# Operand sums of a Strassen product moved from GpSimd to VectorE, a third tile pair for high and low words, and a new order for the attention stage

## The chip, the cores and the metric

The kernel runs on one core of a Trainium2 chip. The metric is the time of one execution on the device, in microseconds (us). Five engines work side by side, each through its own list of instructions in a fixed order: TensorE (PE, with its weight loads shown as PEld), VectorE (DVE), ScalarE (ACT), GpSimd (POOL) and SyncE (SP), which here only starts transfers (DMA). An instruction waits at the head of its list until what it needs is there, and everything behind it on that engine waits with it.

## The reference

Three parts, one behind the other. In NumPy, cut to what matters:

```python
# 1. attention with hashed buckets: q, k, v are 2 x 8 x 768 x 64, proj is 64 x 6
q_bits, k_bits = (q @ proj > 0), (k @ proj > 0)              # 6 bits each -> a bucket number
mask   = q_bucket[:, :, :, None] == k_bucket[:, :, None, :]
scores = where(mask, q @ k.T / 8, -1e9)
attn   = exp(scores - rowmax);  attn /= attn.sum(-1) + 1e-9
x = (attn @ v)  -> 1536 tokens x 512
# 2. gated layer: w1, w2 512 x 1024, w3 1024 x 1024, w_out 1024 x 512
x = ((x @ w1) * (x @ w2)) @ w3 @ w_out
# 3. four experts, mixed by p = domain_probs / sum: e1 4 x 512 x 1024, e2 4 x 1024 x 512
out = sum_e p[:, e] * (relu(x @ e1[e]) @ e2[e])
```

## The kernel before

Every float32 operand of a matmul is cut into a high word (a copy rounded to the type that TensorE reads fast) and a low word (the rest), and a product is three matmuls: high by high, high by low, low by high. The high word is an ACT copy (`hi_of`, line 155), the low word a DVE subtraction (`lo_of`, line 158), or either on POOL (`pool_hi`, 161; `pool_lo`, 164).

No engine order is written out by hand. Each step is an `op(key, engine, duration, function, dependencies, priority)`, and `emit_all` walks all steps with a list planner: each engine takes, of what is ready by the planned durations, the step with the lowest priority number. `RANK`, a table with a number for each kind of step of the attention stage, is added to the priorities; `LAT` holds the planned delays from engine to engine. What comes out is each engine's fixed list. So a changed number in `RANK`, in `LAT` or in a planned duration moves instructions but adds none.

**Attention** (about the first 272 us). 16 heads, each of three units of 256 queries. A unit is: two score matmul groups into one of two PSUM tiles `s_ps`; the row minimum of the negated scores on DVE, which also copies them to SBUF (`e`, line 426); the exponential on ACT (429); a small sum on POOL and a reciprocal on DVE (442, 444); the scaling on POOL or ACT (438, 439); three rounds of transposes on PE into `t_ps` (460), high words on ACT (466) and low words on DVE (468); the product with v into `pv_ps`; an ACT copy (485) and a DVE sum (487) into the token tile `xa`. Each head is prepared ahead (`head`, 324 to 362): q and k rows are loaded into `r`, scaled and cut on POOL (`hh`, `ll`), and copied by DMAs into `ka`, `kb` and `hh`; v is loaded into `rv`, in rows of 64 numbers, and cut on POOL. The hash bits come from a matmul (`bits_of`), a comparison on DVE (`is_pos`, 377) and, for all heads but the first, DMAs (400, 402) that put them under the scores' operands, where they act as the mask. For head 0 the comparisons write straight to the operands (`first_head`: keys `mk` and `mq`).

Beside the attention the weights of part 2 are prepared (`conv64`, 181 to 216): they come as 64-bit numbers, a raw tile `wraw` of 512 KB each (196), and an ACT instruction (198) and five DVE instructions make one float32 half tile of them in `cbuf`; the first eight halves are then cut on ACT and POOL, the later ones on ACT and DVE. ACT's instruction of line 198 waits for the landing of its raw tile. When enough of the first 512 tokens is done, 96 matmuls of part 2 fill gaps of TensorE at the end of the stage.

**Parts 2 and 3** (from 274 us). TensorE runs twelve matmuls a group: gate products, then `w3` by `w_out`, then the layer H in three blocks of 512 tokens. Each of a block's eight groups of H needs one pair of high and low words in a ring of two tiles (`hl`). Block 0 lands in the PSUM tiles `o_ps`, block 1 in `u_ps`, block 2 in `o_ps`. Part 3 multiplies the first two blocks by a Strassen scheme of seven products (`mul`, products m = 1 to 7); five of these need sums or differences of quarters of H's output. In the kernel before, ACT copies all of blocks 0 and 1 from PSUM to the SBUF tiles `G` (eight copies), and POOL makes ten sums of 128 x 512 from them (line 859: two for each of the products 4, 3, 1, 7, 6) into `cbuf`; ACT and DVE then cut each sum into high and low words (`split`). This happens while TensorE runs block 2 (470 to 500 us). In the same stretch POOL also cuts expert weights (161, 164, tiles of 128 x 1024). The four experts follow.

## Time and profile before

| | us |
|---|---|
| runs (median of 3; 1002.5 to 1004.2) | 1002.8 |
| the profiled execution | 1005.64 |
| its span in the trace | 1003.9 |
| PE busy | 977.6 (97%) |
| DVE busy | 662.0 (66%) |
| ACT busy | 432.4 (43%) |
| POOL busy | 313.4 (31%) |

PE is idle for 26.3 us of the span. The page's slices show which engines are full where: in the first quarter (attention) DVE and ACT are nearly as full as PE, and the transfers are dense in the first 50 us; from there on PE alone is full, but for the slice from 477 to 502 us. The granted clock of TensorE is at its full level, 2.4 GHz, in all slices. Times of rows count from the start of the span; `[0.71 <-PE s_ps L149]` at a row's end says that the engine stood idle for 0.71 us ahead of it and what ended that.

### The profile page before, as it was taken

What the parts mean: (1) busy time and instruction counts of PE and PEld (TensorE: products, weight loads), DVE (VectorE), ACT (ScalarE), POOL (GpSimd) and SP (SyncE); (2) the same over time, 40 slices, a digit from 0 to 9 for tenths busy, and PEclk for the clock granted to TensorE, in tenths of its full rate; (3) what the DMA queues carried; (4) which work ended last, traced back from release to release, by engine and by line L of the source; (5) the groups of instructions that cost most, each with busy time, mean ns of one, the idle gap of its engine ahead of it and who ended that gap; (6) DMA issues with size and microseconds to landing.
All of it is one profiled execution on the core that took longest, in us unless ns stands there. A gap on an engine that the chain in (4) does not pass through costs nothing.

```text
span 1003.9 us, 13346 instructions
## 1 busy us (share of the span) xinstructions
PE 977.6 (97%) x4939; PEld 822.7 (82%) x4939; DVE 662.0 (66%) x1194; ACT 432.4 (43%) x779; POOL 313.4 (31%) x297
## 2 busy tenths in 40 slices
PE   7899999999999999999799999999999999999998
PEld 6788888988788888888588888888888888888886
DVE  6799999998499984954965444554445544455343
ACT  5789999988533332434422221222212222122121
POOL 6777788764000000041641204212042120421000
PEclk9999999999999999999999999999999999999999
DMA  5853554321033331320210101101011010100012
GB/s 159 192 130 79 130 122 107 93 61 42 1 105 121 124 113 39 109 84 1 63 43 26 38 1 57 49 26 39 0 59 48 27 37 1 57 28 21 1 50 77
DMA packets 51137, 64.13 MB, mean 64 GB/s; under 512 B 17688, under 2 KB 34072, under 8 KB 51072
## 3 DMA queue, kind: packets, MB, share of 16 engines
q1 hardware_dynamic: 50928, 63.27, 22.1%
q8 instruction: 39, 0.64, 0.3%
q14 instruction: 26, 0.21, 0.1%
q10 hardware_dynamic: 144, 0.01, 0.0%
...
## 4 chain that ended last, share of the span: by engine, by line
PE 73%; DVE 18%; ACT 3%; issue 2%; DMA 2%; POOL 1%; SPq 0%; DVEq 0%; ACTq 0%
PE u_ps L149 50%; PE o_ps L149 19%; DVE et L468 5%; DVE e L426 5%; PE t_ps L149 2%; DMA r<-in_qk 1%; ACT e L429 1%; DVE xa L487 1%; PE pv_ps L149 1%; PE t_ps L460 1%; PE s_ps L149 1%; ACT et L466 1%; DVE hl L158 1%; DVE xh L158 1%; DVE hl L876 1%
## 5 line engine op out<-in xcount | busy, mean ns | idle before, releaser
L149 PE MATMUL u_ps<-xh,slot 128*128 128x512 f32 x768 | 179.9, 389 | 1.2 <-DVE xh L158 1.2
L149 PE MATMUL o_ps<-slotl,hl 128*128 128x512 f32 x768 | 178.2, 390 | 0.4 <-DVE hl L876 0.2
L149 PEld LDWEIGHTS u_ps<-xh,slot 128*128 128x128 f32 x768 | 144.1, 188 | 31.5 <-DVE xh L158 1.6
L149 PEld LDWEIGHTS o_ps<-slotl,hl 128*128 128x128 f32 x768 | 143.9, 188 | 31.5 <-DVE hl L876 1.7
L881 DVE TENSOR_TENSOR m<-m,u_ps 128x512 f32<-128x512 f32 x96 | 62.9, 683 | 138.4 <-ACT m L155 114.7
L161 POOL TENSOR_SCALAR slot<-wraw 128x1024 fp32r<-128x1024 f32 x16 | 17.3, 1080 | 384.6 <-DVE slotl L158 184.1
L149 PE MATMUL u_ps<-xh,slotl 128*128 128x512 f32 x480 | 111.6, 389 | 0.0
L149 PEld LDWEIGHTS u_ps<-xh,slotl 128*128 128x128 f32 x480 | 90.1, 188 | 18.7
L468 DVE TENSOR_TENSOR et<-t_ps,et 128x512 fp32r<-128x512 f32 x144 | 96.5, 680 | 5.3 <-ACT et L466 4.7
L429 ACT ACTIVATE e<-e,sm 128x768 f32<-128x768 f32 x96 | 89.6, 934 | 12.3 <-DVE e L426 10.8
L426 DVE TENSOR_SCALAR_CACHE_REDUCE e<-s_ps 128x768 f32<-128x768 f32 x96 | 90.3, 945 | 4.3 <-PE t_ps L460 3.1
L149 PE MATMUL pv_ps<-et,vv 128*128 128x256 f32 x576 | 91.8, 295 | 0.9 <-DVE xa L487 0.7
L460 PE MATMUL t_ps<-ident,e 128*128 128x128 f32 x576 | 85.6, 276 | 6.7 <-DVE et L468 4.8
L466 ACT ACTIVATE et<-t_ps 128x512 fp32r<-128x512 f32 x144 | 83.0, 593 | 12.5 <-PE t_ps L460 5.8
L149 PE MATMUL u_ps<-slotl,hl 128*128 128x512 f32 x384 | 87.7, 389 | 0.0
L149 PEld LDWEIGHTS u_ps<-slotl,hl 128*128 128x128 f32 x384 | 72.1, 188 | 15.0
L460 PEld LDWEIGHTS t_ps<-ident,e 128*128 128x128 f32 x576 | 65.2, 140 | 16.9 <-DVE et L468 7.9
L149 PEld LDWEIGHTS pv_ps<-et,vv 128*128 128x128 f32 x576 | 75.0, 190 | 3.4 <-DVE xa L487 2.8
L439 POOL TENSOR_SCALAR e<-e,sm 128x768 f32<-128x768 f32 x72 | 65.7, 921 | 18.4 <-DVE sm L444 15.0
L155 ACT ACTIVATE m<-u_ps 128x512 f32<-128x512 f32 x32 | 19.1, 598 | 107.0 <-PE u_ps L149 107.0
L873 ACT ACTIVATE hl<-m 128x512 fp32r<-128x512 f32 x32 | 20.3, 633 | 92.3 <-DVE m L881 92.3
L876 DVE SCALAR_TENSOR_TENSOR hl<-gl,hl 128x512 fp32r<-128x512 f32 x32 | 23.8, 742 | 54.3 <-ACT hl L995 46.2
...
## 6 DMA issues: line engine op xcount, KB each, us to landing
...
```

Of the source, the lines that this page charges most:

```text
L149: nc.tensor.matmul(out=o, lhsT=l, rhs=r, start=start, stop=stop)
L155: nc.scalar.activation(out=dst, in_=ps, func=AF.Copy)
L158: nc.vector.tensor_tensor(out=dst, in0=ps, in1=f(hi), op=ALU.subtract)
L426: op(("mx", u, t), "DVE", 873, lambda ps=ps, m=m, e=e: nc.vector.tensor_scalar(out=e, in0=ps[:, 0:S], scalar1=THR, scalar2=None, op0=ALU.m ...
L429: op(("ex", u, t), "ACT", 921, lambda e=e, m=m, rs=rs: nc.scalar.activation(out=e, in_=e, func=AF.Exp, scale=-1.0, bias=m, accum_out=rs), ...
L439: return "POOL", 872, lambda: nc.gpsimd.tensor_scalar(out=e, in0=e, scalar1=r[:, t:t + 1], scalar2=1.0, op0=ALU.mult, op1=ALU.mult)
L460: nc.tensor.transpose(out=ps[:, k, t * 128:(t + 1) * 128], in_=e_t[2 * (u % ER) + t][:, kt * 128:(kt + 1) * 128], identity=ident)
L466: op(("hi", n), "ACT", 480, lambda ps=ps, et=et: nc.scalar.activation(out=et[:, 0], in_=ps, func=AF.Copy), [("T", u, j), ("pv", n - NET)], Tj)
L468: op(("lo", n), "DVE", 602, lambda ps=ps, et=et: nc.vector.tensor_tensor(out=et[:, 1], in0=ps, in1=f(et[:, 0]), op=ALU.subtract), [("hi", ...
L873: op(key, "ACT", 480, lambda: nc.scalar.activation(out=hl_t[n % 2][:, 0], in_=m_t[m], func=AF.Relu), after, clock[0])
L876: op(key, "DVE", 602, lambda: nc.vector.scalar_tensor_tensor(out=hl_t[n % 2][:, 1], in0=src(), scalar=0.0, in1=f(hl_t[n % 2][:, 0]), op0=A ...
L881: nc.vector.tensor_tensor(out=out, in0=a, in1=b, op=o)
```

## The change

- **Sums.** The operand sums of products 4, 3, 1, 7 and 6 are made by DVE. One operand is read straight from the PSUM tile in which H's block lies (`hb`), the other from `G`. Product 4's two sums read block 0's PSUM tile and come during block 1, the other eight read block 1's and come during block 2. ACT copies six quarters to `G` instead of eight. The sums' tiles are `m_t` and `cbuf`, and part 3's products wait for all reads of `u_ps` (`u_in`).
- **Third tile.** The ring `hl` of high and low words has three tiles in part 3; parts before it still use two.
- **v.** The input array v is laid out ahead of the launch so that each partition's row is one piece of 384 numbers (1.5 KB), not six of 64.
- **First mask bits.** For head 0 the second comparison is cut in two, 256 and 512 columns, and the first score group waits for the first piece alone; head 1's low words (key `l`) come behind it.
- **Order.** 32 of the 34 numbers of `RANK` are new, planned durations of transfers are longer (raw tiles 2700 for 1460, heads 2000 for 1130, copies 1000 for 700) with a planned delay of 1900 for 2300, and some planned DVE and ACT durations are longer. The third head's load also waits for more of head 0's steps.

```diff
-    "S0": -59.56,
+    "S0": -145.18,
...
-            ("SP", 1460, [("cd", n - NRAW), ("c2", n - NRAW)], "cl",
+            ("SP", 2700, [("cd", n - NRAW), ("c2", n - NRAW)], "cl",
...
-        "SP": {"PE": 2300, "ACT": 2300, "DVE": 2300, "POOL": 2300, "SP": 2300, "NONE": 0},
+        "SP": {"PE": 1900, "ACT": 1900, "DVE": 1900, "POOL": 1900, "SP": 1900, "NONE": 0},
...
-                op(("l", hh), "DVE", 870, lambda: scaled_lo(nc.vector), [("h", hh)], T, g)
+                op(("l", hh), "DVE", 1000, lambda: scaled_lo(nc.vector), [("h", hh), ("mq", 0)], T, g)
...
-        op(("lv", hh), "SP", 600, lambda: nc.sync.dma_start(out=rv, in_=v[b, h].rearrange("(k p) d -> p k d", p=128)),
+        op(("lv", hh), "SP", 1000, lambda: nc.sync.dma_start(out=rv, in_=v[b, h].rearrange("p (k d) -> p k d", k=NK)),
...
-        op(("mq", 0), "DVE", 865, lambda: is_pos(lo[64:64 + PC], ps, q), [("mk", 0)], T, "b0")
-        keys[("sf", n)] = keys[("mq", 0)]
+        for i, (key, c) in enumerate(((("mq", 0), slice(0, 256)), (("sf", n), slice(256, S)))):
+            op(key, "DVE", (330, 600)[i], lambda c=c: is_pos(lo[64:64 + PC, c], ps, q, c), [("mk", 0)], T + i, "b0")
...
-        hl_t.extend(tiles(2, [128, 2, 512], "hl", F32R, lp))
+        hl_t.extend(tiles(3, [128, 2, 512], "hl", F32R, lp))
...
+    def hl(n):
+        return hl_t[n % (2 if n < KF * NB else 3)]
...
-    def xs(m):
-        return f(cbuf[:, (4, 3, 1, 7, 6).index(m) % 2])
+    def xs(m, k):
+        return m_t[k + (0 if m == 3 else 2)] if m in (1, 3) else f(cbuf[:, m == 6, k])
...
-        for d in range(KM):
-            op(("hl", blk, d), "ACT", 480, lambda blk=blk, d=d, hb=hb: hi_of(G[blk][:, d], hb[d]),
-               [("H", blk, KF - 1)] + [("gdone", 0, ff) for ff in range(KF)], T)
...
+        kept_d, first_d, m0 = ((0, 1, 2, 3), 0, 2) if blk == 0 else ((2, 3), 2, 5)
+        for d in kept_d:
+            op(("hc", blk, d), "ACT", 480, lambda blk=blk, d=d, hb=hb: hi_of(G[blk][:, d], hb[d]), done, T)
...
-        for m, a, b, o in ((4, x21, x11, ALU.subtract), (3, x12, x22, ALU.subtract), (1, x11, x22, ALU.add),
-                           (7, x21, x22, ALU.add), (6, x11, x12, ALU.add)):
+        sums = ((4, 2, (0, 0), ALU.subtract),) if blk == 0 else (
+            (3, 0, (1, 2), ALU.subtract), (1, 2, (0, 0), ALU.add), (7, 2, (0, 2), ALU.add), (6, 0, (0, 0), ALU.add))
...
-                op(("xs", m, k), "POOL", 1225, lambda m=m, a=a, b=b, o=o, k=k: nc.gpsimd.tensor_tensor(
-                    out=xs(m)[:, k], in0=G[a[0]][:, a[1] + k], in1=G[b[0]][:, b[1] + k], op=o),
+                op(("xs", m, k), "DVE", 602, lambda m=m, a=a, b=b, c=c, o=o, k=k, hb=hb: nc.vector.tensor_tensor(
+                    out=xs(m, k), in0=hb[a + k], in1=G[b][:, c + k], op=o),
```

**What stands in the engines' lists.** Three places follow, before and then after. Number suffixes are buffers.

VectorE, the start of the program: `ll_82` and `ll_83` are the low words of heads 0 and 1, `kb_90` and the 12-row `ll_82` the two comparisons of head 0, `e_96` the first row minimum. Before:

```order
L330 SCALAR_TENSOR_TENSOR ll_82<-r_111,svec,hh_78 128x768
L330 SCALAR_TENSOR_TENSOR ll_83<-r_112,svec,hh_79 128x768
L377 TENSOR_SCALAR kb_90<-s_ps_126,thr,amp 12x768
L377 TENSOR_SCALAR ll_82<-s_ps_126,thr,amp 12x768
L426 TENSOR_SCALAR e_96,sm_119<-s_ps_127 128x768
```

After:

```order
L331 SCALAR_TENSOR_TENSOR ll_82<-r_111,svec,hh_78 128x768
L378 TENSOR_SCALAR kb_90<-s_ps_126,thr,amp 12x768
L378 TENSOR_SCALAR ll_82<-s_ps_126,thr,amp 12x256
L378 TENSOR_SCALAR ll_82<-s_ps_126,thr,amp 12x512
L331 SCALAR_TENSOR_TENSOR ll_83<-r_112,svec,hh_79 128x768
L428 TENSOR_SCALAR e_96,sm_119<-s_ps_127 128x768
```

Head 1's low words moved from ahead of both comparisons to behind them, and the second comparison is two instructions.

ScalarE, around the first instruction that reads a raw weight tile (`cbuf<-wraw_68`). Before it is row 26 of ACT's list, its load row 20 of SP's:

```order
L429 ACTIVATE e_98,sm_123<-e_98,sm_123 128x768
L466 ACTIVATE et_105<-t_ps_129 128x512
L429 ACTIVATE e_99,sm_123<-e_99,sm_123 128x768
L198 ACTIVATE cbuf<-wraw_68 128x512
L466 ACTIVATE et_104<-t_ps_129 128x512
```

After it is row 57, its load row 37:

```order
L468 ACTIVATE et_102<-t_ps_131 128x512
L487 ACTIVATE pvs_107<-pv_ps 64x256
L468 ACTIVATE et_103<-t_ps_129 128x512
L199 ACTIVATE cbuf<-wraw_68 128x512
L431 ACTIVATE e_96,sm_122<-e_96,sm_122 128x768
```

The instruction moved back by 31 rows and its load by 17.

VectorE in the last block of H: `hl` are low words for H's groups, `xh`, `slot` and `slotl` the low words of Strassen operands, `cbuf`, `m` the sums. Before:

```order
L158 TENSOR_TENSOR hl_3029<-xa,hl_3029 128x512
L158 TENSOR_TENSOR xh_3019<-gl_3027,xh_3019 128x512
L158 TENSOR_TENSOR xh_66<-cbuf,xh_66 128x512 x2
L158 TENSOR_TENSOR xh_3019<-cbuf,xh_3019 128x512
L158 TENSOR_TENSOR hl_3030<-xa,hl_3030 128x512
L158 TENSOR_TENSOR xh_3019<-cbuf,xh_3019 128x512
L158 TENSOR_TENSOR hl_3029<-gl_3028,hl_3029 128x512
L158 TENSOR_TENSOR slot_62<-cbuf,slot_62 128x512
L158 TENSOR_TENSOR hl_3030<-gl_3028,hl_3030 128x512
```

After:

```order
L158 TENSOR_TENSOR hl_3031<-xa,hl_3031 128x512
L158 TENSOR_TENSOR xh_3020<-gl_3028,xh_3020 128x512 x2
L158 TENSOR_TENSOR xh_3020<-m_3034,xh_3020 128x512
L158 TENSOR_TENSOR hl_3030<-xa,hl_3030 128x512
L864 TENSOR_TENSOR m_3035<-u_ps_3041,gl_3028 128x512
L158 TENSOR_TENSOR slot_62<-m_3036,slot_62 128x512
L158 TENSOR_TENSOR slot_62<-m_3037,slot_62 128x512
L158 TENSOR_TENSOR xh_3020<-m_3035,xh_3020 128x512
L158 TENSOR_TENSOR hl_3031<-xa,hl_3031 128x512
L864 TENSOR_TENSOR cbuf<-u_ps_3042,g_67 128x512
L864 TENSOR_TENSOR cbuf<-u_ps_3043,g_67 128x512
L158 TENSOR_TENSOR hl_3030<-gl_3029,hl_3030 128x512
```

Eight sums (line 864) now stand in this list between H's low words; two subtractions, those of product 4, left it for block 1.

## Rows read from the trace of the kernel before

**Rows 1.** Waits of PE: engine, line, releaser: us in total, times, longest us.

```profile
PE o_ps L149 <- DVE hl L158: 5.2, 5, 1.5
PE o_ps L149 <- DVE hl L876: 0.2, 1, 0.2
```

**Rows 2.** Busy us by stretch: us, PE, PEld, DVE, ACT, POOL, PEclk, DMA share, GB/s.

```profile
25.00:50.00 25.00, 20.58 (x148) 18.54 (x147) 19.84 (x43) 19.25 (x39) 19.86 (x23) 1.00 0.85 194
100.00:150.00 50.00, 48.66 (x355) 44.31 (x354) 49.52 (x107) 46.73 (x93) 40.16 (x48) 1.00 0.52 125
350.00:400.00 50.00, 50.00 (x222) 41.40 (x222) 31.09 (x58) 13.28 (x23) 0.00 (x0) 1.00 0.23 74
450.00:500.00 50.00, 44.85 (x193) 35.48 (x192) 36.00 (x37) 22.14 (x38) 22.85 (x13) 1.00 0.09 25
260.00:265.00 5.00, 5.00 (x29) 4.38 (x28) 1.79 (x4) 0.58 (x2) 0.00 (x0) 1.00 0.00 0
```

**Rows 3.** Timeline of the start: start us, us, engine, line, operation [idle before]; then one tile's group.

```profile
8.02 0.28 PE L149 MATMUL s_ps<-ll,pbh 128*128 128x256 f32 x1
9.92 1.08 DVE L377 TENSOR_SCALAR kb<-s_ps,thr,amp 12x768 fp32r<-12x768 f32 x1
11.03 1.07 DVE L377 TENSOR_SCALAR ll<-s_ps,thr,amp 12x768 fp32r<-12x768 f32 x1
12.81 0.96 DVE L426 TENSOR_SCALAR_CACHE_REDUCE e<-s_ps 128x768 f32<-128x768 f32 x1 [0.71 <-PE s_ps L149]
...
L330 DVE SCALAR_TENSOR_TENSOR ll<-r,svec,hh x2: 1019/1699/2379, 6.4 to 7.5; 128x768 fp32r<-128x768 f32 x2
```

**Rows 4.** Timeline, 15 to 42 us: POOL, then DVE after its long gaps.

```profile
15.83 0.90 POOL L351 TENSOR_SCALAR r<-r,svec 128x768 f32<-128x768 f32 x1
17.11 1.84 POOL L164 TENSOR_TENSOR ll<-r,hh 128x768 fp32r<-128x768 f32 x1
19.34 2.68 POOL L439 TENSOR_SCALAR e<-e,sm 128x768 f32<-128x768 f32 x3
22.35 0.17 DVE L444 RECIPROCAL sm<-sm 128x2 f32<-128x2 f32 x1 [2.04 <-POOL sm L442]
33.51 0.43 DVE L200 TENSOR_SCALAR cbuf<-cbuf 128x512 f32<-128x512 f32 x1 [1.67 <-ACT cbuf L198]
41.84 0.96 DVE L426 TENSOR_SCALAR_CACHE_REDUCE e<-s_ps 128x768 f32<-128x768 f32 x1 [2.78 <-PE t_ps L460]
```

**Rows 5.** Timeline: raw tile loads on SP, ACT's first reads of them, DVE behind.

```profile
26.34 0.43 SPq L196 DMA_DIRECT2D wraw<-in_w  x1
32.79 0.68 ACT L198 ACTIVATE cbuf<-wraw 128x512 f32<-128x512 f32 x1 [1.47 <-DMA wraw<-in_w]
62.50 0.37 SPq L196 DMA_DIRECT2D wraw<-in_w  x1
68.24 0.67 ACT L198 ACTIVATE cbuf<-wraw 128x512 f32<-128x512 f32 x1 [2.12 <-DMA wraw<-in_w]
69.43 0.69 DVE L468 TENSOR_TENSOR et<-t_ps,et 128x512 fp32r<-128x512 f32 x1 [1.73 <-ACT et L466]
```

**Rows 6.** Timeline in and behind the last block of H: POOL and DVE.

```profile
478.44 2.85 POOL L164 TENSOR_TENSOR slotl<-wraw,slotl 128x1024 fp32r<-128x1024 f32 x1
478.96 2.88 DVE L158 TENSOR_TENSOR xh<-cbuf,xh 128x512 fp32r<-128x512 f32 x1
481.25 6.82 POOL L859 TENSOR_TENSOR cbuf<-g,gl 128x512 f32<-128x512 f32 x4
502.44 2.64 DVE L881 TENSOR_TENSOR m<-m,u_ps 128x512 f32<-128x512 f32 x4 [0.54 <-PE u_ps L149]
503.25 2.41 POOL L164 TENSOR_TENSOR slot<-wraw,slot 128x1024 fp32r<-128x1024 f32 x1
```

**Rows 7.** Stretches of half a microsecond, columns as in the second group.

```profile
165.00:165.50 0.50, 0.50 (x5) 0.50 (x5) 0.50 (x1) 0.48 (x3) 0.50 (x1) 1.00 0.99 395
205.00:205.50 0.50, 0.50 (x7) 0.50 (x6) 0.50 (x3) 0.50 (x2) 0.00 (x0) 1.00 0.96 219
```

More of the change, by code (lines that the diff above doesn't have):

```diff
@@ L27 @@
     "CP": 16.1,
[L28 to L59 removed]
+    "S0": -145.18,
+    "S1": -25.65,
+    "T0": -239.96,
+    "T1": -102.2,
+    "T2": -154.22,
+    "b0": 25.44,
+    "b1": -195.19,
+    "bits": -112.79,
+    "en": -239.65,
+    "ex0": 16.57,
+    "ex1": -26.35,
+    "fd": -190.81,
+    "fx": 57.64,
+    "hi0": 26.3,
+    "hi1": -174.65,
+    "hi2": -42.43,
+    "ld": -147.73,
+    "lo0": 1.38,
+    "lo1": -154.39,
+    "lo2": -137.92,
+    "lv": -113.67,
+    "mx0": -252.86,
+    "mx1": -28.91,
+    "p0": -23.78,
+    "p1": -102.39,
+    "po": -95.03,
+    "prep": -35.61,
+    "pv": -23.28,
+    "r1": -46.45,
+    "r2": -72.09,
+    "v": 25.95,
+    "xa": -161.97,
 }
@@ L675, in take_hl @@
         nh[0] += 1
[L676 removed]
+        return n, ([("hf", n - (2 if n < KF * NB + 2 else 3))] if n > 1 else sw)
     def down(key, n, lhs, rhs, first, last, after, ps=None):
@@ L849, in split @@
             op(("xd", m, k), "DVE", 602, lambda: lo_of(bx(m)[:, 1, k], src(), bx(m)[:, 0, k]), [("yh", m, k)], TX)
+        done = [("H", blk, KF - 1)] + [("gdone", 0, ff) for ff in range(KF)]
+        kept_d, first_d, m0 = ((0, 1, 2, 3), 0, 2) if blk == 0 else ((2, 3), 2, 5)
+        for d in kept_d:
+            op(("hc", blk, d), "ACT", 480, lambda blk=blk, d=d, hb=hb: hi_of(G[blk][:, d], hb[d]), done, T)
         for k in range(2):
-            split(m, k, lambda blk=blk, d=d + k: G[blk][:, d], [("hl", blk, d + k)] + after)
@@ L927, in go @@
                         mm(u_ps[n % 4], lhs()[:, a, k], bx(m)[:, b, k], i == 0, i == 5)
-                op(("M", e, fp, m), "PE", 6 * 227, go, free_ + after + [("xd", m, k) for k in range(2)], clock[0])
+                op(("M", e, fp, m), "PE", 6 * 227, go, free_ + u_in + after + [("xd", m, k) for k in range(2)], clock[0])
                 clock[0] += Q / 2
@@ L944, in tile_lsh_attention_moe @@
                 n, got = mul(m, lhs, have_u)
-                op(("uf", n), "ACT", 480, lambda n=n, x=x: hi_of(m_t[x], u_ps[n % 4]), got + prev, clock[0])
+                op(("uf", n), "ACT", 480, lambda n=n, x=x: hi_of(m_t[x], u_ps[n % 4]), got + prev + [("xd", 3, k) for k in range(2)], clock[0])
                 keys[key(f"t{m}")] = keys[("uf", n)]
```

111 lines of the change are left out of this document (41 added, 70 removed).

## The prediction

> **What bounds the kernel now.** I read the waits of PE first, since PE is the fullest engine, then the busy times by stretch, then the timeline wherever a stretch showed gaps. Two stretches lose time.
>
> From 274 us on PE is the bound and full: 350 to 400 us shows 50.00 busy of 50, 222 matmuls, so one is 50 / 222 = 0.225 us and a group of twelve 2.70 us [rows 2]. The one hole is 450 to 500 us, with 44.85 busy [rows 2]: PE waits there five times, 5.2 us in sum, for DVE's line 158, H's low words [rows 1]. DVE is late because it advances in step with POOL: a DVE subtraction of 128 x 512 started at 478.96 and took 2.88 us, ending 0.55 us behind a POOL instruction that ran from 478.44 for 2.85 us; POOL's sums follow each other at 6.82 / 4 = 1.70 us [rows 6].
>
> In the attention stage PE shows busy, but DVE sets the pace: from 100 to 150 us DVE is busy 49.52 of 50 and PE 48.66 [rows 2]. Before 72 us DVE has holes. Four are long: 2.04, 1.67 and 2.78 us [rows 4] and 1.73 us [rows 5]; with the slow start, they are what can be gained there, because behind 72 us DVE has hardly any. At the end PE takes over: 260 to 265 us shows PE 5.00 of 5 and DVE 1.79 [rows 2].
>
> **The change part by part.** The profiled execution took 1005.6 us, its span 1003.9 and 1.7 around it; the median of the runs is 1002.8, so I carry a difference over to that, 2.8 us lower. The granted clock is at full in every stretch [rows 2] and gets no term.
>
> *First mask bits.* Bits of head 0 leave PE at 8.02 + 0.28 = 8.30. In the kernel before DVE first makes head 1's low words, 2.38 us against 1.02 for head 0's, and starts the comparisons at 9.92 and 11.03; the first row minimum comes at 12.81 [rows 3]. After, the comparisons can start at 8.35: 1.11 us for the first (the step from 9.92 to 11.03), some 0.40 and 0.75 for the two pieces of the second (a third and two thirds of 1.07, and an instruction's fixed part). Scores run on PE from 9.9 on, beside the rest. Then come head 1's low words, 1.02 to 2.38 us by the two rows, and the first minimum, at 11.6 to 13.0. POOL is at work there too, so I take 1.3 us: 11.9, a gain of 0.9 (bounds -0.2 and 1.2). Their copy to `ka` on SP comes later, behind two loads of q, k and one of v; nobody needs it before head 1's scores.
>
> *POOL at the first units.* DVE's reciprocal at 22.35 waited 2.04 us for a POOL addition, which stood behind three scalings from 19.34 on, and these behind head 2's subtraction (17.11, 1.84 us) and head 3's first scaling (15.83, 0.90 us) [rows 4]. In POOL's new list head 3's scaling stands behind the first of the three, so this one starts at least 0.9 us earlier; it can't return more than the 2.04. I take 1.3 (0.9 to 2.0).
>
> *Raw weight tiles.* ACT waited 1.47 us for the first tile, loaded at 26.34 and read at 32.79, and 2.12 us for the third, loaded at 62.50 and read at 68.24; DVE behind it 1.67 [rows 4] and 1.73 us [rows 5]. A load so takes up to 6.4 us in this stretch. The order after has the first load 17 places later on SP and its reader 31 places later on ACT, the second load three rows behind it and its reader at ACT's row 65. The load's predecessor on SP copies head 5's low words; when these were done in the trace, ACT stood near row 35, 22 rows ahead of the new reader, and a row of ACT is 46.73 / 93 = 0.50 us [rows 2]: some 11 us, enough. I book 1.5 of the 1.67 (1.2 to 1.7) and 1.5 of the 1.73 (0.5 to 1.7; I compared the rows of the first two tiles alone). What was hidden by these holes comes due later: DVE has the same 40 instructions of conversion in its list before the last sum of attention in both orders, so nothing is added.
>
> *Copies of head 3.* The 2.78 us at 41.84 [rows 4] end when the first score of head 3 is there, whose bits and copies waited in transfers: DMA is 0.85 busy from 25 to 50 us [rows 2]. What leaves this queue is one 512 KB tile, and v costs less: 196.6 KB of v in 256-byte rows move at 219 / 0.96 = 228 GB/s, 0.86 us, loads with 2 and 3 KB rows at 395 / 0.99 = 399 GB/s, 0.49 us for v and 1.3 us for the tile [rows 7]. So about 1.7 us of traffic go from ahead of the copies, against six small transfers on SP that stay as they were. I take 1.3 (0 to 2.5).
>
> Sum of attention: 0.9 + 1.3 + 1.5 + 1.5 + 1.3 = 6.5 us (2.4 to 9.1). Does it reach the end? Behind 72 us DVE works without holes through the same instructions, plus one, so its stream keeps the lead; at 230 us PE takes over with as many matmuls as before, of which 38 instead of 51 are left behind the last product with v. Seven of DVE's conversion instructions stand behind the 82nd of 96 row minima instead of ahead of it, where DVE has gaps: up to 7 x 0.65 = 4.5 us more, not booked, since PE is at 48.66 of 50 and can hardly go faster.
>
> *Sums on DVE.* POOL loses ten instructions of 1.70 us, ACT two copies. DVE gets ten of 0.66 us, if a sum with an operand in PSUM costs what line 881's do: four of them took 2.64 us while POOL subtracted beside them [rows 6]. In block 2 (eight groups, 8 x 2.70 = 21.6 us) DVE then has 8 low words, 10 subtractions, 8 sums and five small ones, 26 x 0.66 + some 2 = 19 us: it fits. The low words for the group after next have 2.70 us less an ACT copy and a subtraction (0.68 + 0.69 [rows 5]) and the handovers between the engines, some 0.4: 0.9 us of slack. Two expert weight tiles are still cut on POOL in this block. If a 2.85 us subtraction of them holds up H's low words, it costs PE 2.85 - 0.9 = 1.95 us each time, if not, nothing: 0 to 3.9 us remain, I take 2.3. The stage gains 5.2 - 2.3 = 2.9 us (1.3 to 5.2). Part 3's products wait for all reads of `u_ps`; the last sum stands two low words ahead of the group before which the first product runs, so this wait is covered; uncovered it would cost one sum, 0.7 us.
>
> *Third tile.* PE's wait for part 3's low words is 0.2 us [rows 1]; I book 0.2 (0 to 0.4).
>
> Total 6.5 + 2.9 + 0.2 = 9.6 us: 1005.6 - 9.6 = 996.0 for a profiled execution, **993.2** for the median.
>
> **The rivals.**
> 1. *POOL's weight cuts take the place of its sums.* The rows show one DVE subtraction held for the whole of a POOL instruction [rows 6]. If both remaining tiles meet H's low words, the stage keeps 3.9 us: 993.2 + 1.6 = 994.8. For it: the tiles become due by H's groups, in the middle of the block. Against: in the rows the DVE instruction started 0.52 us behind POOL's; started ahead it would have run. On this the Trainium skill, "SBUF — State Buffer", section "SBUF: two separate sides", says that VectorE with two SBUF inputs and GpSimd hold a port pair in turn, for a whole instruction, whoever starts first. By that rule the 3.9 us come about only if POOL starts first both times, and the trace agrees for the one case (2.88 us, where a subtraction of this size takes 0.69).
> 2. *The early holes come back elsewhere.* Transfers stay dense, the first minimum gets its 13.0, the copies of head 3 still arrive late, and the new lists put small waits in. Attention gains 1 us instead of 6.5: 993.2 + 5.5 = 998.7. For it: DMA at 0.85 [rows 2]. Against: two of the four holes are ACT waiting for a raw tile, and these the order plainly removes.
> 3. *Slower: the reciprocal waits for POOL in every head.* In the new lists DVE's reciprocal must find POOL's addition done; POOL makes a head's low words in 1.84 us at one piece, and where the addition is queued behind it DVE stands, as at 22.35, where it cost 2.04 us [rows 4]. 13 heads follow. At 0.9 us a head (11.7 us) the gain of 9.6 is gone by more than 2; at 1.1 us a head it is 993.2 + 14.3 = 1007.5. For it: nearly all priorities are new and DVE has no slack. Against: POOL's new list keeps the addition's place around the low words (subtraction, addition, scaling) as in the old one, and such a wait came only three times before.
> 4. *No change*: attention loses about 2 us in new waits instead of gaining 6.5 and the H stage gains what it should: 1002.8 + 2 - 3.1 = 1001.7.
>
> **How the numbers follow.** Two runs of this kernel differ by about 0.2%, 2.0 us, so faster means below 1000.8 and slower above 1004.8. Chances: forecast 0.52, rival 1 0.15, rival 2 0.15, rival 4 0.08, rival 3 0.10. The first three are faster: 0.82. The range: both stages at their better bounds give 1002.8 - 9.1 - 5.2 - 0.4 = 988.1, and part of the unbooked 4.5 us below that, so 987; above, it takes in rival 2 with its spread and most of rival 4, 1001.5, and leaves out rival 3.
>
> **What would show it.** In the profile after: the first row minimum at 11.6 to 12.2 us; no wait of ACT for `wraw` over 0.5 us before 100 us; the sum of DVE's idle time from 10 to 72 us near 4 us instead of 10; part 2's first `u_ps` matmul near 266 us instead of 272; PE's wait for line 158 between 0 and 3.9 us, with POOL's line 164 beside what remains; DVE's sums near 0.66 us. It is wrong if the sums take over 1 us, if DVE is held for POOL in the steady stretch (100 to 150 us busy below 48), or if the gain at 72 us is lost by 272.

## The result and the profile after

The changed kernel takes 993.94 us in the median of four runs (993.85 to 994.16), the kernel before 1003.06 (1002.5 to 1004.2) beside it: a ratio of 0.9908, with a 95% interval of 0.9891 to 0.9925. The forecast was 993.2. The time came out near it, and inside the range, though all three parts of the sum were of another size than written: attention gained more, the sums less, the third tile more, and a loss of 1.3 us came that was not forecast. The span of the profiled execution is 992.0 us, 11.9 less than that of before.

PE's waits after, to be laid beside [rows 1] (engine, line, releaser: us in total, times, longest us). The wait for DVE's line 158 (H's low words) has gone from five pieces to three and from 5.2 to 4.0 us only; the wait for line 876 (part 3's low words, the one that the third `hl` tile is for) has gone; a wait for ACT is new:

```profile
PE o_ps L149 <- DVE hl L158: 4.0, 3, 2.6
PE o_ps L149 <- ACT slotl L155: 0.7, 1, 0.7
```

Busy times by stretch after, columns as in [rows 2]. From 25 to 50 us PE went from 20.58 to 25.00 and DVE from 19.84 to 23.33; from 100 to 150 us both are as full as before; from 450 to 500 us PE has 46.05 instead of 44.85:

```profile
25.00:50.00 25.00, 25.00 (x188) 23.56 (x187) 23.33 (x51) 23.23 (x48) 22.67 (x29) 1.00 0.72 197
100.00:150.00 50.00, 48.48 (x354) 44.67 (x355) 49.42 (x106) 46.08 (x91) 39.84 (x48) 1.00 0.43 106
450.00:500.00 50.00, 46.05 (x201) 37.18 (x200) 36.88 (x54) 20.03 (x34) 14.22 (x8) 1.00 0.13 43
```

The start after (timeline: start us, us, engine, line, operation, idle before in brackets), which answers to [rows 3]. The first comparison starts at 8.03, the two pieces of the second follow, head 1's low words start at 10.43 and take 1.02 us, and the first row minimum is at 11.36 instead of 12.81:

```profile
8.03 1.08 DVE L378 TENSOR_SCALAR kb<-s_ps,thr,amp 12x768 fp32r<-12x768 f32 x1 [1.27 <-PE s_ps L149]
9.14 1.25 DVE L378 TENSOR_SCALAR ll<-s_ps,thr,amp 12x256 fp32r<-12x256 f32 x2
10.43 1.02 DVE L331 SCALAR_TENSOR_TENSOR ll<-r,svec,hh 128x768 fp32r<-128x768 f32 x1
11.36 0.95 DVE L428 TENSOR_SCALAR_CACHE_REDUCE e<-s_ps 128x768 f32<-128x768 f32 x1
```

What became of the long gaps of [rows 4] and [rows 5]: the longest wait for POOL's addition left in this stretch is 0.44 us, and the first raw tile is loaded at 42.77 and read at 49.63 with no wait ahead of it (nothing in brackets):

```profile
27.23 0.17 DVE L446 RECIPROCAL sm<-sm 128x2 f32<-128x2 f32 x1 [0.44 <-POOL sm L444]
42.77 0.58 SPq L197 DMA_DIRECT2D wraw<-in_w  x1
49.63 0.69 ACT L199 ACTIVATE cbuf<-wraw 128x512 f32<-128x512 f32 x1
```

Block 2 of H after, which answers to [rows 6]: PE's three waits, POOL's two weight cuts, and DVE's instructions beside them. A sum of DVE with an operand in PSUM takes 0.69 us (two in 1.28). DVE's subtractions with both operands in SBUF take 4.16 us for two (1.37 and 2.86) and 2.81 for one, each ending some 0.55 us behind an instruction of POOL's weight cuts:

```profile
464.35 5.74 PE L149 MATMUL o_ps<-hl,slotl 128*128 128x512 f32 x24 [0.20 <-DVE hl L158]
472.64 5.74 PE L149 MATMUL o_ps<-hl,slotl 128*128 128x512 f32 x24 [2.56 <-DVE hl L158]
479.57 5.51 PE L149 MATMUL o_ps<-hl,slotl 128*128 128x512 f32 x23 [1.20 <-DVE hl L158]
...
467.00 1.06 POOL L161 TENSOR_SCALAR slotl<-wraw 128x1024 fp32r<-128x1024 f32 x1 [28.49 <-PE o_ps L149]
468.14 2.69 POOL L164 TENSOR_TENSOR slotl<-wraw,slotl 128x1024 fp32r<-128x1024 f32 x1
475.29 1.20 POOL L161 TENSOR_SCALAR slotl<-wraw 128x1024 fp32r<-128x1024 f32 x1 [4.46 <-PE o_ps L149]
476.58 2.39 POOL L164 TENSOR_TENSOR slotl<-wraw,slotl 128x1024 fp32r<-128x1024 f32 x1
...
467.22 4.16 DVE L158 TENSOR_TENSOR slot<-m,slot 128x512 fp32r<-128x512 f32 x2
472.50 1.28 DVE L864 TENSOR_TENSOR cbuf<-u_ps,g 128x512 f32<-128x512 f32 x2
475.51 1.28 DVE L864 TENSOR_TENSOR cbuf<-u_ps,g 128x512 f32<-128x512 f32 x2
476.71 2.81 DVE L158 TENSOR_TENSOR hl<-gl,hl 128x512 fp32r<-128x512 f32 x1
```

### Where the time went, by stretch

PE passes a few places that are the same in all these kernels, so each trace can be cut there. *Arrival* is the start of ACT's first high words of head 0, which wait for the first loads. *A* runs from there to the first full product into `u_ps` (273.97 us in the kernel before), *B* from there to the first group of block 1, *C* over blocks 1 and 2 to the second product of part 3, *D* from there to the start of DVE's last four sums. In us, each a difference of two starts in the timeline, with the median of the runs:

| kernel | arrival | A | B | C | D | runs |
|---|---|---|---|---|---|---|
| before | 5.41 | 268.56 | 174.00 | 51.55 | 498.58 | 1003.06 |
| before, again | 5.65 | 266.20 | 173.97 | 51.53 | 498.68 | 1004.99 |
| after | 4.77 | 259.19 | 175.23 | 49.81 | 497.28 | 993.94 |
| after, again | 4.98 | 259.35 | 175.28 | 50.00 | 497.28 | 994.19 |
| v256 | 5.50 | 259.17 | 175.26 | 50.05 | 497.28 | 994.48 |
| swap_l1 | 4.89 | 259.54 | 175.26 | 49.86 | 497.28 | 994.51 |
| old_order | 5.01 | 270.98 | 174.02 | 49.93 | 497.29 | 1004.76 |
| dve_early | 4.83 | 266.31 | 175.28 | 49.82 | 497.28 | 1001.12 |
| dve_late | 4.80 | 266.89 | 175.27 | 49.81 | 497.28 | 1001.88 |
| pool_sums | 4.94 | 259.28 | 175.25 | 51.53 | 497.27 | 995.96 |
| cuts_behind | 5.35 | 259.14 | 175.29 | 45.48 | 497.28 | 990.38 |
| cuts_and_w7 | 5.44 | 259.04 | 173.99 | 46.49 | 497.28 | 989.78 |
| cuts_all | 5.45 | 259.05 | 175.85 | 45.52 | 497.28 | 990.34 |
| two_hl | 4.96 | 259.29 | 175.26 | 49.82 | 498.79 | 995.78 |

Behind attention the stretches repeat to 0.1 us (C to 0.25) unless an edit touches them, so one trace each is enough there. The change against the two traces of before: A 6.9 to 9.4 us shorter, B 1.2 to 1.3 longer, C 1.5 to 1.7 shorter, D 1.3 to 1.4 shorter.

A can be cut once more, at the start of the last of the 96 row minima, in the first trace of before and then in that of after:

```profile
246.85 0.96 DVE L426 TENSOR_SCALAR_CACHE_REDUCE e<-s_ps 128x768 f32<-128x768 f32 x1 [0.18 <-PE s_ps L149]
```

```profile
239.87 0.93 DVE L428 TENSOR_SCALAR_CACHE_REDUCE e<-s_ps 128x768 f32<-128x768 f32 x1
```

From there to the first full product it is 27.1 us in both traces of before and 24.1 in both after. So 3.0 us of A's gain lie behind the last row minimum, and 3.9 to 6.3 ahead of it.

### The profile page after: what moved, and what is told of

It reads as the page before. It is cut to its first block, busy times and chain, and to the rows that moved or that the text cites. A ratio compares the mean times of both kernels' runs of the same rounds, so it can differ in the third digit from the quotient of the medians.

```text
span 992.0 us, 13354 instructions
## 1 busy us (share of the span) xinstructions
PE 973.7 (98%) x4939; PEld 824.7 (83%) x4939; DVE 661.2 (67%) x1205; ACT 431.2 (43%) x777; POOL 296.2 (30%) x287
## 4 chain that ended last, share of the span: by engine, by line
PE 85%; DVE 10%; ACT 3%; issue 2%; POOL 0%; DVEq 0%; POOLq 0%; ACTq 0%
PE u_ps L149 50%; PE o_ps L149 20%; PE s_ps L149 5%; PE pv_ps L149 4%; PE t_ps L462 3%; DVE et L470 3%; DVE e L428 2%; PE t_ps L149 1%; ACT et L468 1%; ACT e L431 1%; DVE xa L489 1%; PE t_ps L517 1%; DVE hl L158 1%; DVE slot L158 0%; ACT pvs L487 0%
## 5 line engine op out<-in xcount | busy, mean ns | idle before, releaser
L149 PE MATMUL pv_ps<-et,vv 128*128 128x256 f32 x576 | 89.2, 293 | 0.8 <-DVE xa L489 0.4
L441 POOL TENSOR_SCALAR e<-e,sm 128x768 f32<-128x768 f32 x72 | 68.6, 960 | 16.9 <-DVE sm L446 15.7
L161 POOL TENSOR_SCALAR slotl<-wraw 128x1024 fp32r<-128x1024 f32 x16 | 17.2, 1078 | 167.8 <-PE o_ps L149 137.4
```

Source lines behind the costliest of these rows:

```text
L149: nc.tensor.matmul(out=o, lhsT=l, rhs=r, start=start, stop=stop)
L161: nc.gpsimd.tensor_scalar(out=o, in0=i, scalar1=1.0, scalar2=1.0, op0=ALU.mult, op1=ALU.mult)
L441: return "POOL", 872, lambda: nc.gpsimd.tensor_scalar(out=e, in0=e, scalar1=r[:, t:t + 1], scalar2=1.0, op0=ALU.mult, op1=ALU.mult)
```

## The experiments

Unless a section says otherwise, a kernel is the changed kernel with the edit shown, and `...` stands for lines of the edit that are left out. Line numbers in some are shifted by a few lines.

### The kernels once more: before_again, after_again

> The kernel before once more, with a trace of its own. Theory: of its time only the attention stage varies. The three stretches behind it are 174.0, 51.55 and 498.58 us again, each within 0.1, and attention, counted from ACT's high words of head 0, differs from the 268.56 us of the first trace by 0.5 us or more, in the waits for transfers ahead of 72 us. Rival: the difference between its executions lies behind attention, and attention is 268.5 within 0.2.

> The changed kernel itself once more, beside its variants on the same chip. Two theories on the start of the first score: if its time of arrival (ACT's high words of head 0 at 4.77, 4.89, 4.94, 5.35 and 5.50 us so far, in kernels with the same first four loads) varies from execution to execution, it lies between 4.7 and 5.6 here, and the stretch from there to the first dense product is 259.2 us again, within 0.1; if the new rows of v bring it forward it is 4.7 to 4.9. The time is 993.5 to 995.

Before: 1004.99 us (1002.59 to 1006.95). In its trace B, C and D are as in the first one and A is 2.36 us shorter, as the theory had it. The gaps of DVE in this second trace of the kernel before:

```profile
22.74 0.17 DVE L444 RECIPROCAL sm<-sm 128x2 f32<-128x2 f32 x1 [2.05 <-POOL sm L442]
32.65 0.43 DVE L200 TENSOR_SCALAR cbuf<-cbuf 128x512 f32<-128x512 f32 x1 [0.41 <-ACT cbuf L198]
40.27 0.96 DVE L426 TENSOR_SCALAR_CACHE_REDUCE e<-s_ps 128x768 f32<-128x768 f32 x1 [2.06 <-PE t_ps L460]
66.89 0.69 DVE L468 TENSOR_TENSOR et<-t_ps,et 128x512 fp32r<-128x512 f32 x1 [0.79 <-ACT et L466]
```

The gap made by POOL is the same to 0.01 us (2.05 for 2.04). The three made by transfers are 0.41, 2.06 and 0.79 where [rows 4] and [rows 5] have 1.67, 2.78 and 1.73: 2.92 us less, which covers the 2.36. So the gaps on which two terms of the prediction stood had another size in each of the two executions. After, again: 994.19 us (993.86 to 994.43), arrival 4.98, A 259.35, 0.05 us outside what the first theory allowed. A hardly varies any more (259.04 to 259.35 in the eight traces that leave it as it is), and nothing in it waits for a raw tile. The time of arrival does vary, from 4.77 to 5.65 us over all kernels with the same first three loads, and from 4.77 to 5.45 in kernels that have the fourth, v, in long rows too.

### v in short rows: v256

```diff
-        op(("lv", hh), "SP", 1000, lambda: nc.sync.dma_start(out=rv, in_=v[b, h].rearrange("p (k d) -> p k d", k=NK)),
+        op(("lv", hh), "SP", 1000, lambda: nc.sync.dma_start(out=rv, in_=v[b, h].rearrange("(k p) d -> p k d", p=128)),
```

(and the input in its old layout; the order on every engine is unchanged)

> The changed kernel, with v read in 256-byte rows as in the kernel before; the order on every engine is that of the changed kernel. Theory: v's short rows hold up the transfers beside them. ACT's high words of head 0 start near 5.4 us instead of 4.77, the first row minimum near 12.0 instead of 11.36, DVE's idle time from 10 to 72 us is 4.3 to 5.5 us instead of 3.7, the time 994.6 to 995.8. Rival: the order alone made the early gain, v's rows nothing. First minimum within 0.15 us of 11.36, the time within 0.3 us of 993.9.

994.48 us (993.86 to 995.79), a little below what the theory asked for and above what the rival did. The first row minimum came at 11.77, between the two as well, and ACT's first high words came late, as the theory had it:

```profile
5.50 0.94 ACT L336 ACTIVATE hh<-r,svec 128x768 fp32r<-128x768 f32 x1 [0.60 <-DMA r<-in_qk]
```

But cuts_behind, with the long rows, shows 5.35 at this place, and counted from the arrival A is 259.17, as in the changed kernel. So the rows of v made no difference behind the arrival. Whether they have a part in the arrival itself is open: with short rows it is 5.41, 5.50 and 5.65 in three traces, with long rows 4.77 to 5.45 in eleven, some half a microsecond at most.

### Head 1's low words ahead of the comparisons: swap_l1

```diff
+        l1, mk = keys[("l", 1)], keys[("mk", 0)]
+        order.remove(l1)
+        order.insert(order.index(mk), l1)
         for i in order:
             ops[i][2]()
```

> The changed kernel, with one instruction of DVE moved: head 1's low words stand ahead of the three mask comparisons again. Theory: POOL's subtraction for head 0 (5.85 to 8.45 us in the changed kernel) holds DVE's subtraction, which would start at 6.8, to 8.45; it ends at 9.2 to 9.5, the comparisons follow, and the first row minimum comes at 11.7 to 12.0 instead of 11.36; the time is 0.3 to 0.6 us longer (994.2 to 994.6). Rival: DVE is not held. Head 1's low words fit into the idle 1.27 us ahead of 8.03, and the first row minimum comes near 10.4, the time near 993.0.

994.51 us (994.38 to 994.64), A 0.2 to 0.35 us longer, and the first row minimum at 11.80, all as the theory had it. DVE's two low-word instructions (third row: shortest, median and longest ns), and POOL beside them:

```profile
5.86 3.52 DVE L334 SCALAR_TENSOR_TENSOR ll<-r,svec,hh 128x768 fp32r<-128x768 f32 x2 [1.31 <-ACT hh L339]
11.80 0.96 DVE L431 TENSOR_SCALAR_CACHE_REDUCE e<-s_ps 128x768 f32<-128x768 f32 x1
...
L334 DVE SCALAR_TENSOR_TENSOR ll<-r,svec,hh x2: 1019/1771/2523, 5.9 to 6.9; 128x768 fp32r<-128x768 f32 x2
...
5.97 2.59 POOL L164 TENSOR_TENSOR ka<-r,hh 64x768 fp32r<-64x768 f32 x1 [4.18 <-ACT hh L339]
```

Head 1's low words start at 6.9, find POOL's subtraction under way until 8.56, and take 2.52 us instead of 1.02. Without a hold they would have fitted into the idle time ahead of the comparisons. So the 2.38 us of [rows 3] were a hold as well, and the new place of the instruction is worth some 0.3 us. Counted from the arrival, the first minimum comes 6.92 us behind it here, 7.40 in the kernel before; what is left, 0.5 us, goes with the split comparison, which was not taken out by itself.

### The order alone: old_order

```diff
-    "S0": -145.18,
+    "S0": -59.56,
...
-        "SP": {"PE": 1900, "ACT": 1900, "DVE": 1900, "POOL": 1900, "SP": 1900, "NONE": 0},
+        "SP": {"PE": 2300, "ACT": 2300, "DVE": 2300, "POOL": 2300, "SP": 2300, "NONE": 0},
```

(all of `RANK`, `LAT` and the planned durations of before)

> The changed kernel, planned with the priorities, planned durations and waits for transfers of the kernel before: the order of the attention stage is made by the old numbers, while the mask comparisons, the rows of v, the sums on DVE and the third tile stay as changed. Theory: the order carries nearly all of the early gain. Attention, counted from ACT's high words of head 0, takes 265.5 to 268.5 us instead of 259.3, the time is 1000.5 to 1003.5. Rival: the rows of v and the mask comparisons carry it, attention takes below 263 us, the time is below 998.

1004.76 us (1003.62 to 1007.34): as slow as the kernel before, and A of 270.98 is even 2.4 to 4.8 us longer than there and longer than the theory had it (265.5 to 268.5). The comparisons, the rows of v and the third head's load gave A nothing without the new numbers. This is not the order of before: under the old numbers the changed steps give another list. In it no instruction of ACT waits for a raw tile ahead of 100 us, DVE has no gap of 2 to 2.8 us at head 3's first score either, but a reciprocal again waits for POOL:

```profile
37.03 0.17 DVE L446 RECIPROCAL sm<-sm 128x2 f32<-128x2 f32 x1 [1.94 <-POOL sm L444]
```

DVE's idle time between 10 us and the last of the 96 row minima (10 us to that start, less the busy time of the stretch) is 13.28 and 10.58 us in the two traces of before, 6.03 and 6.30 after, 12.20 here. So it falls by 4.3 to 7.3 us with the change, which covers the 3.9 to 6.3 us that A loses ahead of the last row minimum. Here 6.1 of the 12.20 lie ahead of 72 us (10.6 and 7.9 before, 3.7 and 4.0 after) and 6.1 behind it (2.7 before, 2.3 after): under the old numbers the early holes are smaller too, but new ones come behind them. Of the 11.7 us by which A is longer here than after, some 6 are this idle time, 3.0 more busy time of DVE, and 2.8 lie behind the last row minimum (26.9 us there). B and C are of use too: B is 174.02 here, so the 1.3 us lost there come with the new numbers, and C is 49.93, so the sums' gain doesn't need them.

### Is a gap at 35 us paid at the end? dve_early, dve_late

```diff
-    ap.tile([128, 272], F32, name="apad")
+    apad = ap.tile([128, 272], F32, name="apad")
...
+        extra = {keys[("mx", u, t)] for u in range(6, 10) for t in range(2)}
         for i in order:
             ops[i][2]()
+            for _ in range(3 * (i in extra)):
+                nc.vector.memset(apad, 0.0)
```

(dve_late: units 44 to 47)

> The changed kernel with 24 idle memsets of DVE added (128 x 272, three behind each of eight row minima, from 35 us on; 0.15 to 0.4 us each). Theory: DVE sets the pace up to 230 us, so a lead gained or lost at 35 us is carried to the end of attention: the end comes later by 0.8 to 1.1 times the busy time of the memsets. Rival: PE sets the pace (48.5 busy of 50), and a part is lost in its slack: less than 0.5 of their busy time.

> The changed kernel with the 24 memsets of dve_early, three behind each of the last eight of the 96 row minima instead of at 35 us. Theory: behind the 88th minimum DVE has idle time and PE sets the pace, so DVE's work there costs little: the end of attention comes later by 0 to 2.3 us (a third of the 6.8 us of memsets). So the seven conversion instructions that the change moves behind the 82nd minimum are worth up to their 4.5 us. Rival: DVE sets the pace to the end, the end comes 6 to 7 us later.

In both the 24 memsets are busy for 6.8 us (busy us, mean ns, idle us before them):

```profile
L293 DVE MEMSET apad<- 128x272 f32 x24 | 6.8, 285 | 2.0
```

Early, they lengthen A from 259.3 to 266.31 us: 7.0 for 6.8, so a gap at 35 us is paid in full; that one that goes is gained in full follows from this, and no run takes one gap away alone. Late, A is 266.89: 7.6 for 6.8. The theory of dve_late falls. DVE sets the pace up to the last row minimum, at 239.87 us in the changed kernel; only behind it does it stand idle for long:

```profile
249.87 1.29 DVE L470 TENSOR_TENSOR et<-t_ps,et 128x512 fp32r<-128x512 f32 x2 [1.01 <-ACT et L468]
258.54 0.69 DVE L600 TENSOR_TENSOR g<-g,t_ps 128x512 f32<-128x512 f32 x1 [3.78 <-PE t_ps L149]
```

### The sums back on POOL: pool_sums

```diff
-                op(("xs", m, k), "DVE", 602, lambda m=m, a=a, b=b, c=c, o=o, k=k, hb=hb: nc.vector.tensor_tensor(
-                    out=xs(m, k), in0=hb[a + k], in1=G[b][:, c + k], op=o),
+                op(("xs", m, k), "POOL", 1225, lambda m=m, a=a, b=b, o=o, k=k: nc.gpsimd.tensor_tensor(
+                    out=xs(m)[:, k], in0=G[a[0]][:, a[1] + k], in1=G[b[0]][:, b[1] + k], op=o),
...
```

(with ACT's eight copies and the sums' tiles of before)

> The changed kernel, with the ten operand sums on POOL out of SBUF copies as in the kernel before; PE's order is that of the changed kernel, and everything ahead of 430 us too. Theory: the sums on DVE gained little, because POOL's two weight cuts hold DVE in their place. PE waits for line 158 5 to 6.5 us instead of 4.0, the time 994.5 to 996.2. Rival (the sum of the prediction): the sums were worth 2.9 us, the time 996.8 or more.

995.96 us (995.95 to 996.14), PE's wait for line 158 is 5.1 us, and C is 51.53, that of the kernel before (51.55 and 51.53). The sums on DVE are worth 1.5 to 1.7 us. In step with POOL's sums DVE's subtractions take 1.77 us each, this one for instance:

```profile
472.75 6.80 POOL L866 TENSOR_TENSOR cbuf<-g,gl 128x512 f32<-128x512 f32 x4
476.63 1.77 DVE L158 TENSOR_TENSOR hl<-gl,hl 128x512 fp32r<-128x512 f32 x1
```

### POOL's weight cuts behind block 2: cuts_behind

```diff
-            if blk == NB - 1 and ff in (1, 3, 7):
-                load_o(0, min((ff + 1) // 2, 3), [("H", blk, ff - 1), ("H", blk, ff)])
+            if blk == NB - 1 and ff == 7:
+                for fp in (1, 2, 3):
+                    load_o(0, fp, [("H", blk, ff - 1), ("H", blk, ff)])
```

> The changed kernel, with the cutting of expert 0's second, third and fourth down tile on POOL made to wait for the last group of H; the order on PE, DVE and ACT is that of the changed kernel. Theory: these cuts hold DVE's low words. PE's wait for line 158 falls from 4.0 us to 0.4 or less, the two DVE subtractions of 2.8 and over 3 us are back at 0.69, and the time is 989.8 to 990.8. Rival: DVE has too much to do in this block (26 instructions in 21.6 us) and is late by itself. 2 us or more of the wait stay, the time is 992 or more.

990.38 us (989.98 to 991.02). C falls from 49.8 to 45.48. Of PE's 4.0 us 0.2 remain, and 71 matmuls run through:

```profile
464.93 16.41 PE L149 MATMUL o_ps<-hl,slotl 128*128 128x512 f32 x71 [0.20 <-DVE hl L158]
...
450.00:500.00 50.00, 49.80 (x220) 40.84 (x220) 35.70 (x56) 21.61 (x37) 10.29 (x6) 1.00 0.09 26
```

DVE has the same instructions in the same order in this block and is not late by itself: the two cuts of POOL were 3.8 of the 4.0 us.

### The last product of the fused weights earlier: cuts_and_w7, cuts_all

In the changed kernel the last product of `w3` by `w_out` stands directly ahead of the last group of block 0, which reads it; before, a group stood between them:

```profile
432.50 2.88 PE L149 MATMUL u_ps<-slot,slot 128*128 128x512 f32 x12
436.07 3.29 PE L149 MATMUL o_ps<-hl,slotl 128*128 128x512 f32 x12 [0.69 <-ACT slotl L155]
439.19 22.01 PE L149 MATMUL u_ps<-hl,slotl 128*128 128x512 f32 x96
```

PE waits 0.69 us, and the group takes 439.19 - 436.07 = 3.12 us from start to start instead of 2.72. That is 1.09 of the 1.3 us by which B grew.

```diff
-                 lambda d, b, n=n: hl(n)[:, b], ff == 0, ff == KF - 1, [("gl", n), ("wl", ff), ("H", blk, ff - 1)] + bank_free, hb)
+                 lambda d, b, n=n: hl(n)[:, b], ff == 0, ff == KF - 1, [("gl", n), ("wl", ff), ("H", blk, ff - 1)] + ([("W", KF - 1)] if (blk, ff) == (0, KF - 2) else []) + bank_free, hb)
```

> The kernel of cuts_behind, in which also the last product of the fused weights stands two groups of H ahead of the group that reads it, instead of one, as in the kernel before. Theory: the new wait of PE on ACT's line 155 (0.7 us) and the slower group behind it (3.29 instead of 2.88 us) go: the stretch from the first dense product to block 1 is 174.0 to 174.2 us instead of 175.26, the time 988.7 to 989.6. Rival: the 1.2 us have another cause (block 0's sums on DVE) and stay: 175 or more, the time 990 or more.

989.78 us (989.51 to 991.19). B is 173.99, but C grew from 45.48 to 46.49 and took most of it back, so the time is just above what the theory had. The low words for block 1's first group now come while POOL makes the first expert's, and DVE is held there; PE has done one matmul of the block when it waits for them:

```profile
436.30 2.40 POOL L164 TENSOR_TENSOR slotl<-wraw,slotl 128x1024 fp32r<-128x1024 f32 x1
...
436.62 2.63 DVE L158 TENSOR_TENSOR hl<-xa,hl 128x512 fp32r<-128x512 f32 x1 [2.06 <-ACT hl L155]
...
439.30 22.19 PE L149 MATMUL u_ps<-hl,slotl 128*128 128x512 f32 x95 [0.44 <-DVE hl L158]
```

```diff
-    load_u(0, 0, [("W", KF - 1)], [("H", NB - 1, 5), ("W", KF - 1)])
-    load_o(0, 0, [("W", KF - 1)])
+    load_u(0, 0, [("H", 1, 2)], [("H", NB - 1, 5), ("W", KF - 1)], [("gl", KF + 4)])
...
```

(the last list holds back the subtraction; the first down tile goes with the three others)

> The kernel of cuts_and_w7, in which the two remaining weight cuts of POOL near block 0's end move too: expert 0's first down tile waits for the last group of H, and the subtraction of its first up tile for a low word of DVE in the middle of block 1. Order of PE, DVE and ACT as in cuts_and_w7. Theory: DVE's low words that took 2.63 us at 436.6 in that kernel were held by POOL's subtraction from 436.3 on (2.40 us), and this ate the 1.29 us gained ahead of it. They are back at 0.69, blocks 1 and 2 take 45.2 to 45.8 us instead of 46.49, the time is 988.4 to 989.3. Rival: block 1 loses them in another way, since the moved subtraction holds DVE there, 46.3 us or more, the time 989.6 or more.

990.34 us (990.08 to 990.69), a miss. C is 45.52, as expected, but B is 175.85. The subtraction did not move into block 1: the dependence I gave the planner orders lists, it is no wait on the chip. With nothing in front of it on POOL it ran as soon as its data was there, and held another DVE subtraction, for which PE waited:

```profile
429.22 2.68 POOL L164 TENSOR_TENSOR slot<-wraw,slot 128x1024 fp32r<-128x1024 f32 x1
...
429.71 2.75 DVE L217 TENSOR_TENSOR slot<-slot,cbuf 128x512 fp32r<-128x512 f32 x1
...
432.51 2.56 PE L149 MATMUL u_ps<-slot,slot 128*128 128x512 f32 x10 [1.53 <-DVE slot L217]
```

In cuts_behind the edit works because the cuts stand behind an instruction on POOL that truly waits, the first one of the second up tile, which waits for PE until 482.80 us. The three kernels are within 0.6 us of each other, and the best, cuts_and_w7, is 4.4 us faster than the changed kernel beside it (994.19) and 0.9864 (0.9848 to 0.9879) of the kernel before.

### Two tiles again: two_hl

```diff
-        return hl_t[n % (2 if n < KF * NB else 3)]
+        return hl_t[n % 2]
...
-        return n, ([("hf", n - (2 if n < KF * NB + 2 else 3))] if n > 1 else sw)
+        return n, ([("hf", n - 2)] if n > 1 else sw)
```

> The changed kernel, with two tiles instead of three for high and low words in part 3; the order on every engine stays. Theory: the third tile gained 1.3 us, about 0.3 to 0.4 in each of the four experts, though the waits of PE before showed 0.2 alone: the stretch from the second product of part 3 to DVE's last sum is 498.4 to 498.7 us instead of 497.28, the time 995.0 to 995.5. Rival (the prediction): 0.2 to 0.4 us, the stretch is below 497.8.

995.78 us (995.46 to 996.48), D 498.79, both a little above the theory: the third tile is worth 1.5 us. PE's list is that of the changed kernel; the lists of ACT and DVE in part 3 are not, the planner made them anew for two tiles (the last 300 instructions of DVE stand as in the kernel before), so the 1.5 us belong to the tile together with these lists. The waits of PE for part 3's low words show 0.6 us in this kernel and showed 0.2 before. The rest is inside groups, which the timeline shows by their length. The end of the first expert before, then after, 96 matmuls from start to start:

```profile
601.52 22.32 PE L149 MATMUL o_ps<-slotl,hl 128*128 128x512 f32 x96
623.68 0.62 PE L149 MATMUL u_ps<-xh,slot 128*128 128x512 f32 x2
```

```profile
591.00 21.92 PE L149 MATMUL o_ps<-slotl,hl 128*128 128x512 f32 x96
612.76 2.88 PE L149 MATMUL u_ps<-xh,slot 128*128 128x512 f32 x12
```

22.16 us against 21.76, with no pause long enough to be listed as a wait. Three of the four experts end so, in 22.16, 22.15 and 22.27 us before and in 21.76 each after (the third with a listed wait of 0.21): 1.3 us, the whole of D's gain.

## Why the prediction was right, point by point

**The total, 9.6 us, carried over to a median 2.8 us lower.** The sum was made against an execution of 1005.6 us and taken off the median. The changed kernel's profiled execution (993.85 us) does not differ from its median (993.94), so against that execution the gain is 11.8 us and against the median 9.1. The second trace of before shows why: the first had longer gaps in front of transfers. By the table the terms are, against the second trace, 6.85 for attention, -1.31 and 1.53 for B and C, 1.40 for the third tile, 8.5 in sum; against the first 9.37, -1.23, 1.74 and 1.30, 11.2 in sum, and 0.64 of earlier arrival. Carrying the difference over was not right. What made the profiled execution long was in part the gaps that the change takes away, so the changed kernel has no such excess: with each term as large as it proved in the execution from which it was read, 11.8 us, the forecast would have been 1002.8 - 11.8 = 991.0. That it came within 0.8 us is luck: the sum was 2.2 us too small for its execution, and the carrying over took off 2.8 us that the changed kernel does not show. Inside the sum, too, errors met: the sums on DVE were 1.2 to 1.4 us too large and a loss of 1.3 was left out, while attention and the third tile were too small by 1.5 to 4.0 together.

**Attention, 6.5 us: the mechanism right in the main, the size 6.9 to 9.4**, by the trace of before that one takes. That a lead at 35 us is carried to the end is shown (dve_early, 7.0 for 6.8). The five parts all lie early; counted from the arrival, the last row minimum came 3.9 to 6.3 us earlier, where 6.5 was forecast, and the 3.0 us behind it stand in no term. Part by part:
- *First mask bits*, 0.9: from the arrival to the first row minimum 7.40 and 7.41 us before, 6.59 and 6.26 after, so 0.8 to 1.15. Right. But only some 0.3 of it is head 1's low words (swap_l1).
- *POOL at the first units*, 1.3: the one gap that is the same in both traces of before, 2.04 and 2.05 us; it is gone after, and the next reciprocal waits 0.44 and 0.62 us in the two traces. Right, and POOL's list is as said: head 3's scaling at 18.05 stands between the first two of the three.
- *Raw weight tiles*, 1.5 and 1.5: the waits are gone, as said. What they were worth was read from one execution; in the second they were 0.41 and 0.79.
- *Copies of head 3*, 1.3: the gap (2.78, then 2.06) is gone. The working, 1.7 us less traffic, is not borne out: the gap is gone with v in short rows as well (v256), and under the old numbers with the first tile loaded as early as before, at 25.24 us (old_order). Which part of the change took it away is open; the third head's load, which waits for more in both, was not taken out.
- *PE takes over at 230 us*: wrong. DVE sets the pace to 240 us, and the seven late conversions, up to 4.5 us not booked, are no reserve (dve_late, 7.6 for 6.8). What PE does gain at the end are fillers done earlier: from the first matmul behind the last product with v to the first full product it takes 273.97 - 261.85 = 12.12 us before and 263.96 - 253.72 = 10.24 after, 1.9 of the 3.0 us. The count was read wrongly: the traces have 46 fillers there before and 39 after, not 51 and 38.

**Sums on DVE, 2.9 us: 1.5 to 1.7** (C, and pool_sums). The price of a sum, 0.66, was right (0.69 alone, two in 1.28). The step that failed is the choice of 2.3 between 0 and 3.9 for POOL's two weight cuts. Both held DVE, and PE paid 2.56 + 1.20 = 3.76 (4.0 with a first 0.20, which cuts_behind still has), where rival 1 had put 3.9. It was not 1.95 each time: the first tile's two instructions of POOL held one subtraction each. The blocks gained 1.5 to 1.7, the lower part of the bounds of 1.3 to 5.2; cuts_behind gains 4.3 to 4.5 more. I had argued that a DVE instruction that starts ahead of POOL's would run. That is so (in swap_l1 head 0's low words started at 5.86, 0.11 us ahead of POOL's subtraction, and took 1.02 us), but DVE has one such subtraction after another here, and in each of the three holds of this block the next one started 0.1 to 0.4 us behind a start of POOL's. On the rule that the prediction weighed, from the Trainium skill, "SBUF — State Buffer", section "SBUF: two separate sides", the traces agree in each place: the held subtractions started at 476.71, 436.62 and 429.71, behind POOL's at 476.58, 436.30 and 429.22, and ended behind POOL's end. The page names two SBUF inputs as the condition, and the trace after agrees there too: a subtraction with one operand in PSUM ran in 0.69 us while POOL subtracted,

```profile
433.77 2.39 POOL L164 TENSOR_TENSOR slot<-wraw,slot 128x1024 fp32r<-128x1024 f32 x1
436.11 2.40 POOL L164 TENSOR_TENSOR slotl<-wraw,slotl 128x1024 fp32r<-128x1024 f32 x1
...
436.05 0.69 DVE L158 TENSOR_TENSOR slotl<-u_ps,slotl 128x512 fp32r<-128x512 f32 x1 [4.71 <-ACT slotl L155]
```

The sums of block 2 point the same way, as far as they met POOL: the two from 475.51 on ran beside its line 161 (475.29, 1.20 us) and took 1.28 us together, while the subtraction at 467.22, beside the same kind of instruction (467.00, 1.06 us), took 1.37. Seven of the ten sums had nothing of POOL beside them.

The 1.3 us lost in B were not in the prediction at all: I compared no rows of the order there. They come with the new numbers (old_order has 174.02) and not with the sums (pool_sums has 175.25), and they go when the last product of the fused weights stands one group earlier (cuts_and_w7, 173.99); which number moves the product is open.

**Third tile, 0.2 us: 1.3 to 1.5.** The step that failed is to take the list of waits for the loss: the ends of three experts lost 0.4 to 0.5 us each, of which the list of before has 0.2 in all.

**The rivals.** Rival 1 came true for its part: the stage kept 4.0 us of waits. Rivals 2 and 4 did not: the early holes did not come back, DVE's idle time from 10 to 72 us is 3.7 us. Rival 3 did not: the reciprocal's waits for POOL in all of attention fell from 3.6 us to 1.2 (idle time ahead of line 444, now 446).
